# Sums of weight blocks moved from the operands' preparation into the weights' decoding, for three layers, and a later place in the queue for one token block

## The chip, the cores and the metric

The kernel runs on one core of one Trainium2 chip. The metric is device time in microseconds (us) of one execution; lower is better. Five engines work at once, each through its own instructions in a fixed order: TensorE (PE, matrix products), VectorE (DVE), ScalarE (ACT), GpSimd (POOL) and SyncE (SP), which here issues every DMA. An instruction that waits holds back all that stand behind it on its engine.

## The reference, cut to what matters

```python
x = attention(q, k, v)          # linear attention, 8 x 576 tokens, 512 wide -> x[4608, 512]
h = x @ w_in                    # 512 -> 2048
x = np.maximum(0.01 * h, h) @ w_out          # first MLP, 2048 -> 512
h = x @ w_in2                   # second MLP
out = (h * (1.0 / (1.0 + np.exp(-h)))) @ w_out2
```

The four weight matrices reach the core as 64-bit floats; the kernel turns their bits into 32-bit floats itself ("decoding"). Everything else is 32-bit.

## The kernel before, in words

**Layers and tiles.** The 4608 tokens are cut into nine token blocks `j` of 512. Layer 0 (the *plain layer*) is `x @ w_in` with 16 weight tiles `f`, run beside the attention. Layers 1, 2 and 3 are `w_out`, `w_in2` and `w_out2`. They are computed block by block with seven products in place of eight: an operand is seen as 2x2 sub-blocks, sums and differences of them are formed, and seven products `c` = 1..7 are made for each token block `j` and group `i` (four groups, `NG = 4`), always in the order `ORDER = (1, 2, 6, 7, 5, 3, 4)`. One product is 12 matmuls of 128x256, since each operand is kept as a rounded high part and a low part and three of their four combinations are summed. Below, (8,2) means token block 8, group 2.

**How an operand is made** (`operand`, `fetch`, `sums`, `split2`). Each of the seven needs a *room*, a buffer of 128x1024. Some of the seven are loaded from DRAM into their room (`fetch`, an SP DMA); the others are sums of loaded ones (`sums`, DVE, line 819, through the helper `add`). Then each is split: ACT copies it rounded into the room's first half (line 298), DVE subtracts this and writes the low part into the second half (line 294). A product can start when the DVE subtraction of both its operands is done. Weights have 28 rooms of their own (tiles `a0` to `a27`), one for each group and product; a room passes to the next layer when the last token block has used it. Token operands share 12 rooms in `r_x` (tiles `x00` to `x13`, `g`, `xs`), taken in order of need and returned after the product. Layer 1 and 3 need seven token operands for every group; layer 2 seven for a whole token block, used by all four groups.

**What comes out.** The seven products stand in PSUM banks (tiles `b`, `h`; eight in all) and are added up by `blocks`: one copy on ACT, then seven additions on DVE (line 819, `o<-o,b` and `o<-o,h`), each of which frees or helps to free a bank. In layer 1 they are written to DRAM (`x2d`) and loaded again as layer 2's token operands by `x_all`.

**Decoding the weights** (`convert`, `convert1` to `convert3`). One 128x512 tile is one 512 KB load into one of two `raw` buffers, two ACT copies (lines 331, 346) and four DVE instructions (lines 333, 337, 342, 348). Layers 1 and 2 write the decoded tile to DRAM (`w1d`, `w2d`); both buffers of `r_raw` are in use, one for the bits and one for the result. Their sums are made later, when the operand is prepared: four DVE additions of 128x512 for each group, 16 for each layer. Layer 3 (`convert3`) already makes the sums while decoding, on two tiles at a time, as four additions of 128x256 (line 410), and writes seven blocks to `w2c`, from which all seven operands are loaded. `convert2` begins when all of `convert1` is done; `convert3` when all of `convert2` is done and the last token block of layer 1 is near.

**What sets the order.** No engine chooses at run time. A planner in the kernel's code (`Queues.run`) walks through tasks, gives each operation a planned cost and picks the one that can start first; among equals the lower `rank` goes first. What it picks is written to the engines in that order. Rooms and buffers go to whoever asks first. The rank of layer `l`, block `j`, group `i` is

```python
def step2(layer, j, i):
    return NB * NF + (((layer - 1) * NB + j) * NG + i) * 2
```

so one group is two ranks. `g_all` asks for token rooms 4 ranks ahead of a group's products, `x_all` 10 ranks ahead of a token block's, the weights 8 ranks ahead.

Of the kernel before, what the change touches and what calls it, by code (L numbers as in the profile page):

```python
# [26 lines left out]
def v_tt(n):  # L27
    return 0.16 + n / 960
# [30 lines left out]
def get(ring):  # L59
    return "get", ring  # L60


class Queues:
# [26 lines left out]
    def done(self, key):  # L90
        self.events[key] = self.now
# [111 lines left out]
def linear_attention_two_mlps(  # L203
# [24 lines left out]
    nc = tc.nc  # L228
    B, H, S, D = q.shape
    NT, DM = out.shape  # L230
    DFF = w_in1.shape[1]
    P = 128
# [26 lines left out]
    w2d = tc.dram_tile([NF, P, DM], F32, name="w2d")  # L259
    w1d = tc.dram_tile([NF, P, DM], F32, name="w1d")  # L260
    w2c = tc.dram_tile([NF // 2, P, 7, DM // 2], F32, name="w2c")
# [55 lines left out]
    def load_bits(dst, l, o, f):  # L317
        yield op(("D", 1.46))
        if not o:
            dst = dst.rearrange("p (k m) -> p k m", k=KD)  # L320
        nc.sync.dma_start(out=dst, in_=w_bits(l, o, f))
# [43 lines left out]
        r_o.put(t)  # L365
        done(("w", f))

    def convert(l, o, dst, name, r):

        for f in range(NF):  # L370
            yield rank(r(f))
            raw = yield get(r_raw)
            bits = raw.bitcast(U32)
            yield from load_bits(bits, l, o, f)
            t = yield get(r_raw)
            yield from decode(bits, t[:, 0:DM], DM)
            r_raw.put(raw)
            yield op(("D", 0.73))
            nc.sync.dma_start(out=dst[f], in_=t[:, 0:DM])
            yield wait()  # L380
            r_raw.put(t)
            done((name, f))

    def convert1():
        yield wait(("l1", 1, NF - 1))
        yield from convert(0, 1, w1d, "w1", lambda f: step(3, 0) + 4 * f)

    def convert2():
        yield wait(*(("w1", f) for f in range(NF)))
        yield from convert(1, 0, w2d, "w2", lambda f: step2(1, f // 3, 0) - 4)  # L390

    def convert3():

        yield wait(*(("w2", f) for f in range(NF)), ("p", 1, NB - 2, NG - 1, 1))
        n = DM // 2
        for r in range(NF // 2):
            yield rank(step2(2, r, 0) - 4)
            t = yield get(r_raw)
# [6 lines left out]
            b = {1: t[:, 0:n], 5: t[:, n:2 * n], 2: t[:, 2 * n:3 * n], 3: t[:, 3 * n:4 * n]}  # L405
            u = yield get(r_raw)
            o = {c: u[:, i * n:(i + 1) * n] for i, c in enumerate((4, 5, 6, 7))}
            for dst, x, y in ((o[7], b[3], b[5]), (o[5], b[5], b[1]), (o[6], b[3], o[5]), (o[4], b[2], o[6])):
                yield op(("V", v_tt(n)))
                nc.vector.tensor_tensor(out=dst, in0=x, in1=y, op=ALU.subtract)  # L410
            yield op(("D", 0.73))
            nc.sync.dma_start(
                out=w2c[r, :, 0:2], in_=t.rearrange("p (c e n) -> p c e n", c=2, e=2)[:, :, 0]
            )
            yield op(("D", 0.73))
            nc.sync.dma_start(out=w2c[r, :, 2], in_=b[3])
            yield op(("D", 0.73))
            nc.sync.dma_start(out=w2c[r, :, 3:7], in_=u.rearrange("p (c n) -> p c n", c=4))
            yield wait()
            r_raw.put(t)  # L420
            r_raw.put(u)
            done(("w2c", r))

    def w_of(f):
        return wtiles[f].rearrange("p t (k m) -> p t k m", k=KD)
# [329 lines left out]
    def lend(c):  # L755
        return (yield get(r_x))

    def weights(l, i, srcs, kind, order):
# [15 lines left out]
    def weights1(i):  # L774
        w = w1d[4 * i:4 * i + 4].rearrange("(r h) p n -> h p r n", h=2)
        srcs = {
            1: w[0][:, :, 0:HB], 2: w[1][:, :, 0:HB], 5: w[0][:, :, HB:TB], 4: w[1][:, :, HB:TB]
        }
        yield from weights(1, i, srcs, "A", range(1, 8))

    def weights2(i):
        w = w2d[4 * i:4 * i + 4].rearrange("(r h) p n -> h p r n", h=2)
        srcs = {
            1: w[0][:, :, 0:HB], 2: w[0][:, :, HB:TB], 5: w[1][:, :, 0:HB], 4: w[1][:, :, HB:TB]
        }
        yield from weights(2, i, srcs, "A", range(1, 8))

    def weights3(i):
        srcs = {c: w2c[2 * i:2 * i + 2, :, c - 1].rearrange("r p n -> p r n") for c in range(1, 8)}
        yield from weights(3, i, srcs, "", ORDER)  # L790
# [187 lines left out]
    def step(j, f):  # L978
        return place[j, f]

    def step2(layer, j, i):
        return NB * NF + (((layer - 1) * NB + j) * NG + i) * 2

    with tc.manual_schedule():
# [22 lines left out]
            if f < NH:  # L1007
                spawn(f, layer0(0, f))
        spawn(0, layer0_all())
        spawn(1000, convert1())  # L1010
        spawn(1000, convert2())
        spawn(1000, convert3())
        spawn(0, later())
        for i in range(NG):
            spawn(step2(1, 0, i) - 8, weights1(i))
            spawn(step2(2, 0, i) - 8, weights2(i))
            spawn(step2(3, 0, i) - 8, weights3(i))
        spawn(step2(1, 0, 0) - 4, g_all(1))
        spawn(step2(2, 0, 0) - 10, x_all())
        spawn(step2(3, 0, 0) - 4, g_all(3))  # L1020
        spawn(step2(1, 0, 0), layers())
        qs.run()
# [30 lines left out]
```

## Time and profile before

| | |
|---|---|
| median of three runs | 1652.06 us (1650.31 to 1653.68) |
| the profiled execution | 1649.95 us |
| its span, first to last instruction | 1648.2 us |
| PE busy | 1602.6 us, 97% |
| DVE busy | 1185.9 us, 72% |
| ACT busy | 849.4 us, 52% |
| DMA queue of SP, share of 16 engines | 54.2% |

A share of the span is a mean over stages. Layer 0 ends at 528 us, layer 1 at 908, layer 2 at 1280. PE is the engine of the chain that ended last for 92% of the span; its idle time inside the layers is what can be won back, and what a change can add. A row of a timeline gives start and length; in square brackets stands how long the engine was idle before it and what released it.

### The profile page before, as it was taken

What the parts mean: (1) busy time and instruction counts of PE and PEld (TensorE: products, weight loads), DVE (VectorE), ACT (ScalarE), POOL (GpSimd) and SP (SyncE); (2) the same over time, 40 slices, a digit from 0 to 9 for tenths busy, and PEclk for the clock granted to TensorE, in tenths of its full rate; (3) what the DMA queues carried; (4) which work ended last, traced back from release to release, by engine and by line L of the source; (5) the groups of instructions that cost most, each with busy time, mean ns of one, the idle gap of its engine ahead of it and who ended that gap; (6) DMA issues with size and microseconds to landing.
All of it is one profiled execution on the core that took longest, in us unless ns stands there. A gap on an engine that the chain in (4) does not pass through costs nothing.

```text
span 1648.2 us, 30726 instructions
## 1 busy us (share of the span) xinstructions
PE 1602.6 (97%) x11456; PEld 1504.0 (91%) x11456; DVE 1185.9 (72%) x2170; ACT 849.4 (52%) x1824; POOL 41.7 (3%) x56
## 2 busy tenths in 40 slices
PE   6899999999999999999997899999999999999999
PEld 4688888888788999999996899999999999999999
DVE  8986644546335887877778888888879877777775
ACT  5768755676435444444444444444436544444442
POOL 2101000000000000000000000000000000000000
PEclk9999999999999999999997899999999999999999
DMA  8865766564556545444454455555548544444442
GB/s 225 257 187 163 209 184 187 171 206 151 173 169 212 151 152 170 153 135 129 128 168 131 147 176 189 177 179 185 184 157 273 174 132 132 132 135 136 133 137 78
DMA packets 239765, 274.66 MB, mean 167 GB/s; under 512 B 58368, under 2 KB 175104, under 8 KB 239616
## 3 DMA queue, kind: packets, MB, share of 16 engines
q1 hardware_dynamic: 239616, 272.70, 54.2%
q8 instruction: 90, 1.47, 0.4%
q14 instruction: 59, 0.48, 0.1%
HBM read 162.53 MB, written 110.10 MB: 165 GB/s over the span
## 4 chain that ended last, share of the span: by engine, by line
PE 92%; DVE 5%; DMA 1%; issue 1%; ACT 1%; SPq 0%; DVEq 0%; ACTq 0%
PE b L931 22%; PE h L931 21%; PE b L881 10%; PE h L881 10%; PE h L646 8%; PE h L648 8%; PE h L647 8%; PE a L618 2%; PE a L503 2%; DVE o L819 1%; DVE a L294 1%; PE a L603 1%; PE a L504 1%; DVE x L294 0%; DMA raw<-in_moe_w_out_dram 0%
## 5 line engine op out<-in xcount | busy, mean ns | idle before, releaser
L298 ACT ACTIVATE x<-x 128x512 fp32r<-128x512 f32 x211 | 132.9, 631 | 211.6 <-DMA x<-gd 73.1
L646 PE MATMUL h<-x,w 128*128 128x512 f32 x576 | 237.1, 412 | 3.2 <-ACT w L298 2.5
L648 PE MATMUL h<-x,w 128*128 128x512 f32 x576 | 225.5, 391 | 1.2 <-DVE w L294 1.2
L647 PE MATMUL h<-x,w 128*128 128x512 f32 x576 | 224.7, 390 | 0.7 <-DVE x L294 0.7
L819 DVE TENSOR_TENSOR o<-o,h 128x512 f32<-128x512 f32 x190 | 127.5, 686 | 50.3 <-PE h L931 20.2
L819 DVE TENSOR_TENSOR o<-o,b 128x512 f32<-128x512 f32 x188 | 126.3, 686 | 45.7 <-PE b L931 18.6
L679 ACT ACTIVATE o<-h 128x512 f32<-128x512 f32 x144 | 86.1, 598 | 139.8 <-PE h L648 135.6
L931 PE MATMUL b<-a,x 128*128 128x256 f32 x1104 | 141.6, 283 | 0.0
L893 ACT ACTIVATE o<-o 128x512 f32<-128x512 f32 x144 | 87.8, 627 | 103.8 <-DVE o L819 103.6
L294 DVE TENSOR_TENSOR x<-x 128x512 fp32r<-128x512 f32 x211 | 138.7, 685 | 2.4
L298 ACT ACTIVATE x<-o 128x512 fp32r<-128x512 f32 x166 | 103.7, 631 | 65.8 <-DVE o L819 46.3
L931 PE MATMUL b<-x,a 128*128 128x256 f32 x1008 | 129.5, 286 | 8.1 <-DVE x L294 8.1
L931 PEld LDWEIGHTS b<-a,x 128*128 128x128 f32 x1104 | 136.5, 192 | 0.3 <-DVE x L294 0.2
L646 PEld LDWEIGHTS h<-x,w 128*128 128x128 f32 x576 | 108.4, 188 | 29.7 <-ACT w L298 3.3
L881 PE MATMUL b<-x,a 128*128 128x256 f32 x1044 | 134.8, 285 | 0.0
L931 PEld LDWEIGHTS b<-x,a 128*128 128x128 f32 x1008 | 125.9, 195 | 8.3 <-DVE x L294 8.3
L648 PEld LDWEIGHTS h<-x,w 128*128 128x128 f32 x576 | 108.1, 188 | 25.7 <-DVE w L294 2.5
L881 PE MATMUL h<-x,a 128*128 128x256 f32 x1020 | 130.9, 283 | 0.0
L881 PEld LDWEIGHTS b<-x,a 128*128 128x128 f32 x1044 | 130.1, 194 | 0.0
L647 PEld LDWEIGHTS h<-x,w 128*128 128x128 f32 x576 | 108.4, 188 | 22.5 <-DVE x L294 1.4
L931 PE MATMUL h<-x,a 128*128 128x256 f32 x1008 | 126.8, 283 | 0.0
L881 PEld LDWEIGHTS h<-x,a 128*128 128x128 f32 x1020 | 126.1, 192 | 0.0
(123 smaller groups left out, 2792.0 us busy)
## 6 DMA issues: line engine op xcount, KB each, us to landing
gda<-o SPq DMA_DIRECT2D x144, 256.0 KB, 2.5
gd<-o SPq DMA_DIRECT2D x144, 256.0 KB, 2.8
x<-gd SPq DMA_DIRECT2D x102, 256.0 KB, 2.8
x<-gda SPq DMA_DIRECT2D x90, 256.0 KB, 2.9
raw<-in_moe_w_out_dram SPq DMA_DIRECT2D x32, 512.0 KB, 4.2
g<-gda SPq DMA_DIRECT2D x37, 256.0 KB, 2.7
x2d<-o SPq DMA_DIRECT2D x36, 256.0 KB, 3.2
out_dram<-o SPq DMA_DIRECT2D x36, 256.0 KB, 2.6
```

What stands on the lines that cost most here:

```text
L294: engines[e].tensor_tensor(out=out_, in0=a, in1=b.bitcast(F32), op=ALU.subtract)
L298: nc.scalar.activation(out=out_, in_=in_, func=ACTF.Copy)
L503: nc.tensor.matmul(pk[:, 0:NV], lhsT=kx[:, c * P:(c + 1) * P], rhs=vv[:, c, :], start=c == 0, stop=False)
L618: nc.tensor.matmul(po, lhsT=kv[bb, p], rhs=qT.rearrange("p (c t) -> p c t", c=4)[:, :, a:e], start=True, stop=True)
L646: nc.tensor.matmul(h, lhsT=w[:, 0, kk], rhs=x[:, 0], start=kk == 0, stop=False)
L647: nc.tensor.matmul(h, lhsT=w[:, 0, kk], rhs=x[:, 1], start=False, stop=False)
L648: nc.tensor.matmul(h, lhsT=w[:, 1, kk], rhs=x[:, 0], start=False, stop=kk == KD - 1)
L679: nc.scalar.activation(out=o, in_=h, func=ACTF.Prelu, alpha=0.01)
L819: nc.vector.tensor_tensor(out=o, in0=a, in1=b, op=alu)
L881: nc.tensor.matmul(bank[:, r * HB:(r + 1) * HB], lhsT=w4[:, a, r, k], rhs=x3[:, b, k], start=n == 0, stop=n == 5,)
L893: nc.scalar.activation(out=t, in_=t, func=ACTF.Silu)
L931: nc.tensor.matmul(bank[:, m * HB:(m + 1) * HB], lhsT=s[:, a, at:at + P], rhs=x[:, b, r * HB:(r + 1) * HB], start=i + m + n == 0, stop=i = ...
```

## The change

Three things are altered.

- **Decoding.** `convert` now decodes two tiles, makes four sums of 128x256 at once (line 396 of the changed kernel) and writes all seven blocks to DRAM, for layers 1, 2 and 3 alike (`PLANS`, `wc`). Only the bits stay in `r_raw`; the decoded tiles and the sums take four of the 16 `o` buffers, which hold activations and partial results elsewhere. The second decoder waits for three pairs of the first, the third for three pairs of the second.
- **Weights.** `weights` loads all seven operands of a group and makes no sums. Layer 2's are taken in `ORDER`, as layer 3's already were.
- **Rooms.** `x_all` asks for the rooms of layer 2's first token block 5 ranks ahead of it, not 10, and so after the last `g_all` of layer 1, which asks 6 ranks ahead by the same count.

```diff
+    PLANS = {
+        1: ({1: (0, 0), 2: (1, 0), 5: (0, 1), 4: (1, 1)}, "A", (1, 2, 4, 7, 5, 6, 3)),
+        2: ({1: (0, 0), 2: (0, 1), 5: (1, 0), 4: (1, 1)}, "A", (1, 2, 4, 7, 5, 6, 3)),
+        3: ({1: (0, 0), 5: (0, 1), 2: (1, 0), 3: (1, 1)}, "B", (1, 2, 3, 7, 5, 6, 4)),
+    }
+    def convert(l, r):
+        blocks_of, kind, order = PLANS[l]
         n = DM // 2
-        for r in range(NF // 2):
-            yield rank(step2(2, r, 0) - 4)
-            t = yield get(r_raw)
+        for pair in range(NF // 2):
+            yield rank(r(pair))
+            t = []
             for i in range(2):
                 raw = yield get(r_raw)
                 bits = raw.bitcast(U32)
-                yield from load_bits(bits, 1, 1, 2 * r + i)
-                yield from decode(bits, t[:, i * DM:(i + 1) * DM], DM)
+                yield from load_bits(bits, l // 2, l % 2, 2 * pair + i)
+                t.append((yield get(r_o)))
+                yield from decode(bits, t[i], DM)
                 r_raw.put(raw)
...
+            for i in range(2):
+                u.append((yield get(r_o)))
+                for h in range(2):
+                    dst, x, y, o = SUMS[kind][2 * i + h]
+                    to = u[i][:, h * n:(h + 1) * n]
+                    yield op(("V", v_tt(n)))
+                    nc.vector.tensor_tensor(
+                        out=to, in0=b[x], in1=b[y], op=ALU.add if o == "+" else ALU.subtract
+                    )
+                    b[dst] = to
...
+    def convert1():
+        yield wait(("l1", 1, NF - 1))
+        yield from convert(1, lambda r: step(3, 0) + 4 * r)
+    def convert2():
+        yield wait(("w", 1, 2))
+        yield from convert(2, lambda r: step2(1, r, 0) - 4)
+    def convert3():
+        yield wait(("w", 2, 2))
+        yield from convert(3, lambda r: step2(2, r, 0) - 4)
...
-        key = {1: "w1", 2: "w2", 3: "w2c"}[l]
-        yield wait(*((key, f) for f in (range(2 * i, 2 * i + 2) if l == 3 else range(4 * i, 4 * i + 4))))
-        yield from operand(("w", l, i), kind, step2(l, 0, i) - 8, order, srcs, give)
+        yield wait(("w", l, 2 * i), ("w", l, 2 * i + 1))
...
+        order = range(1, 8) if l == 1 else ORDER
+        yield from operand(("w", l, i), "", step2(l, 0, i) - 8, order, srcs, give)
     def x_all():
         for j in range(NB):
-            r = step2(2, j, 0) - 10
+            r = step2(2, j, 0) - (10 if j else 5)
```

**What the built order shows.** In the rows below a line number of the changed kernel is 9 lower for additions (810 for 819) and 2 lower for splits (292 for 294). Tiles `a` are weight rooms; `x`, `g`, `xs` token rooms; `b`, `h` banks of PSUM; `o` sums.

DVE before, layer 1's last token block: the sums and splits of layer 2's first weight group (rooms `a0` to `a6`), from the last sum to the first split of (8,2), the row of `x03`:

```order
L819 TENSOR_TENSOR o6_159<-a1_3460,o12_165 128x512
L294 TENSOR_TENSOR a0_3459<-a0_3459 128x512
L294 TENSOR_TENSOR a1_3460<-a1_3460 128x512
L819 TENSOR_TENSOR o3_156<-x02_121,x01_120 128x512
L819 TENSOR_TENSOR o9_162<-o3_156,x03_122 128x512
L819 TENSOR_TENSOR o10_163<-g_8505,o3_156 128x512
L294 TENSOR_TENSOR a2_3461<-o6_159,a2_3461 128x512
L294 TENSOR_TENSOR a3_3462<-a3_3462 128x512
L294 TENSOR_TENSOR a4_3463<-o4_157,a4_3463 128x512
L294 TENSOR_TENSOR a5_3464<-o12_165,a5_3464 128x512
L294 TENSOR_TENSOR a6_3465<-o5_158,a6_3465 128x512
L294 TENSOR_TENSOR x03_122<-x03_122 128x512
```

The first product of (8,2) waits for that last row; seven weight splits, four weight sums and three token sums stand ahead of it as one batch.

DVE in the changed kernel, the same weight group:

```order
L292 TENSOR_TENSOR a0_3546<-a0_3546 128x512
L292 TENSOR_TENSOR a1_3547<-a1_3547 128x512
L292 TENSOR_TENSOR a5_3551<-a5_3551 128x512
L810 TENSOR_TENSOR o3_156<-xs_4291,g_8662 128x512
L810 TENSOR_TENSOR o8_161<-o3_156,x10_123 128x512
L810 TENSOR_TENSOR o6_159<-x11_124,o3_156 128x512
L292 TENSOR_TENSOR x10_123<-x10_123 128x512
L292 TENSOR_TENSOR a6_3552<-a6_3552 128x512
L292 TENSOR_TENSOR x11_124<-x11_124 128x512
L292 TENSOR_TENSOR a4_3550<-a4_3550 128x512
L292 TENSOR_TENSOR g_8662<-g_8662 128x512
```

The weight sums are gone, a weight split stands beside a token split, and the first split of (8,2), `x10` on itself, is the seventh row; the splits of layer 2's first token block, which before stood ahead of all these rows, are no longer there.

DVE before, around the first addition of token block 8's outputs (`o6<-o2,b`), in (8,3); `g_8697` is the operand of the third product, `g_8729` of the fourth:

```order
L294 TENSOR_TENSOR x02_121<-x02_121 128x512
L294 TENSOR_TENSOR g_8697<-o7_160,g_8697 128x512
L342 SCALAR_TENSOR_TENSOR raw0_151<-raw1_152,raw0_151 128x512
L819 TENSOR_TENSOR o6_159<-o2_155,b_4156 128x512
L294 TENSOR_TENSOR g_8729<-o11_164,g_8729 128x512
L819 TENSOR_TENSOR o2_155<-o2_155,b_4157 128x512
L294 TENSOR_TENSOR x03_122<-o8_161,x03_122 128x512
```

DVE in the changed kernel, the same place; `g_8823` is the operand of the third product of (8,3), `x10` of the fourth:

```order
L292 TENSOR_TENSOR a10_3556<-a10_3556 128x512
L810 TENSOR_TENSOR o14_167<-o9_162,b_4293 128x512
L292 TENSOR_TENSOR g_8823<-o2_155,g_8823 128x512
L292 TENSOR_TENSOR x10_123<-o4_157,x10_123 128x512
L292 TENSOR_TENSOR x11_124<-o0_153,x11_124 128x512
```

The addition, which needs the second product of (8,3), has moved from behind the third product's split to ahead of it.

DVE before, the last addition of token block 8 (`o4<-o4,h_4750`) and what follows:

```order
L819 TENSOR_TENSOR o4_157<-o4_157,h_4750 128x512
L819 TENSOR_TENSOR o9_162<-o5_158,a14_4485 128x512
L819 TENSOR_TENSOR o14_167<-a15_4503,o9_162 128x512
L333 TENSOR_SCALAR raw0_151<-raw0_151 128x512
L337 TENSOR_SCALAR raw0_151<-raw0_151 128x512
L342 SCALAR_TENSOR_TENSOR raw0_151<-raw1_152,raw0_151 128x512
L294 TENSOR_TENSOR a14_4485<-a14_4485 128x512
L294 TENSOR_TENSOR a15_4503<-a15_4503 128x512
```

DVE in the changed kernel, the last addition (`o5<-o5,h_4958`, fed by the last product of layer 1), and behind it the seven splits of layer 2's first token block:

```order
L810 TENSOR_TENSOR o13_166<-x03_122,o1_154 128x512
L810 TENSOR_TENSOR o5_158<-o5_158,h_4958 128x512
L292 TENSOR_TENSOR x12_125<-x12_125 128x512
L292 TENSOR_TENSOR x13_126<-o15_168,x13_126 128x512
L292 TENSOR_TENSOR g_8910<-g_8910 128x512
L292 TENSOR_TENSOR xs_4291<-o7_160,xs_4291 128x512
L292 TENSOR_TENSOR x00_119<-o1_154,x00_119 128x512
L292 TENSOR_TENSOR x03_122<-x03_122 128x512
L292 TENSOR_TENSOR g_8981<-o13_166,g_8981 128x512
L292 TENSOR_TENSOR a14_4656<-a14_4656 128x512
```

These seven splits (`x12` for product 1, then 5, 3, 7, 6, `x03` for 2, `g_8981` for 4) stood in (8,1) before and now come after the last product of layer 1; the first product of layer 2 needs the first of them, its second product the sixth.

## Rows read from the trace of the kernel before

**Rows 1.** stretches, start:end and length, then busy time by engine
```profile
core 0: us, PE busy (x) PEld busy (x) DVE busy (x) ACT busy (x) POOL busy (x), PEclk, DMA share, GB/s
80.00:528.00 448.00, 448.00 (x2129) 366.93 (x2128) 238.38 (x583) 276.04 (x856) 21.80 (x20) 1.00 0.60 182
528.00:860.00 332.00, 332.00 (x2768) 331.96 (x2767) 257.94 (x418) 158.03 (x259) 0.00 (x0) 1.00 0.51 149
860.00:935.00 75.00, 56.31 (x408) 55.62 (x407) 65.58 (x109) 38.34 (x64) 0.00 (x0) 0.82 0.45 138
```
**Rows 2.** waits of PE, whole span: total us, times, longest
```profile
PE b L931 <- DVE x L294: 8.1, 1, 8.1
...
PE b L881 <- DVE o L819: 6.5, 1, 6.5
...
PE b L931 <- DVE g L294: 4.1, 1, 4.1
...
PE h L931 <- DVE xs L294: 0.5, 1, 0.5
```
**Rows 3.** timeline of PE: start, length, line, tiles, count, [idle before]
```profile
870.88 0.28 PE L931 MATMUL b<-x,a 128*128 128x256 f32 x1
...
898.15 2.76 PE L931 MATMUL b<-x,a 128*128 128x256 f32 x12
...
929.18 2.93 PE L881 MATMUL b<-xs,a 128*128 128x256 f32 x12 [6.51 <-DVE o L819]
...
934.46 1.71 PE L881 MATMUL b<-g,a 128*128 128x256 f32 x11
```
**Rows 4.** chain of waits, layer 1: start, length, engine, count
```profile
528.33 5.75 PE b L931 x48
```
**Rows 5.** timeline of DVE before the first gap
```profile
869.73 1.29 DVE L819 TENSOR_TENSOR o<-a,a 128x512 f32<-128x512 f32 x2
...
878.54 0.68 DVE L294 TENSOR_TENSOR x<-x 128x512 fp32r<-128x512 f32 x1
```
**Rows 6.** timeline of DVE in block (8,3)
```profile
901.02 0.69 DVE L819 TENSOR_TENSOR o<-o,b 128x512 f32<-128x512 f32 x1 [2.42 <-PE b L931]
901.63 0.68 DVE L294 TENSOR_TENSOR g<-o,g 128x512 fp32r<-128x512 f32 x1
```
**Rows 7.** waits of DVE, 860 to 930 us
```profile
DVE o L819 <- PE b L931: 2.4, 1, 2.4
...
DVE o L819 <- DMA x<-gda: 0.2, 1, 0.2
```
**Rows 8.** groups of DVE by form: count, busy us, mean ns
```profile
L342 DVE SCALAR_TENSOR_TENSOR raw<-raw,raw 128x512 uint32<-128x512 uint32 x48 | 33.1, 690 | 1.1
...
L333 DVE TENSOR_SCALAR raw<-raw 128x512 f32<-128x512 f32 x48 | 21.4, 445 | 33.1 <-ACT raw L331 32.4
...
L819 DVE TENSOR_TENSOR o<-a,a 128x512 f32<-128x512 f32 x16 | 10.5, 685 | 1.7 <-DMA a<-w1d 1.7
...
L410 DVE TENSOR_TENSOR raw<-raw,raw 128x256 f32<-128x256 f32 x16 | 6.7, 421 | 0.2
```
**Rows 9.** groups of ACT by form
```profile
L331 ACT ACTIVATE raw<-raw 128x512 f32<-128x512 f32 x48 | 31.9, 664 | 12.8 <-DMA raw<-in_moe_w_out_dram 6.8 <-DMA raw<-in_moe_w_in_dram 5.8
```
**Rows 10.** waits of all engines, 80 to 528 us
```profile
DVE raw L333 <- ACT raw L331: 21.7, 13, 2.8
```
**Rows 11.** DMA issues: count, KB each, median us to landing
```profile
a<-w2c SPq DMA_DIRECT2D x28, 256.0 KB, 4.6
x<-x2d SPq DMA_DIRECT2D x23, 256.0 KB, 4.0
```
**Rows 12.** waits of all engines, whole span
```profile
ACT a L298 <- DMA a<-w2c: 11.0, 8, 3.2
```
**Rows 13.** short stretches, columns as in Rows 1
```profile
50.00:60.00 10.00, 7.30 (x39) 4.75 (x39) 8.60 (x29) 9.28 (x21) 3.37 (x4) 1.00 0.99 309
...
1292.00:1293.00 1.00, 0.47 (x5) 0.27 (x3) 1.00 (x3) 0.11 (x1) 0.00 (x0) 1.00 0.75 201
```

More of the change, by code (lines that the diff above doesn't have):

```diff
@@ L258, in linear_attention_two_mlps @@
     x2d = tc.dram_tile([KD, P, NT], F32, name="x2d")
-    w2d = tc.dram_tile([NF, P, DM], F32, name="w2d")
-    w1d = tc.dram_tile([NF, P, DM], F32, name="w1d")
-    w2c = tc.dram_tile([NF // 2, P, 7, DM // 2], F32, name="w2c")
+    wc = {l: tc.dram_tile([NF // 2, P, 7, DM // 2], F32, name=f"wc{l}") for l in (1, 2, 3)}
     NG = NF // 4
@@ L366, in split1 @@
         done(("w", f))
[L368 to L374, printed above, removed]
-            t = yield get(r_raw)
[L376 to L394, printed above, removed]
+    PLANS = {
[3 rows of a table added]
+    }
+    def convert(l, r):
+        blocks_of, kind, order = PLANS[l]
         n = DM // 2
-        for r in range(NF // 2):
-            yield rank(step2(2, r, 0) - 4)
-            t = yield get(r_raw)
+        for pair in range(NF // 2):
+            yield rank(r(pair))
+            t = []
             for i in range(2):
@@ L401, in convert3 @@
                 bits = raw.bitcast(U32)
-                yield from load_bits(bits, 1, 1, 2 * r + i)
-                yield from decode(bits, t[:, i * DM:(i + 1) * DM], DM)
+                yield from load_bits(bits, l // 2, l % 2, 2 * pair + i)
+                t.append((yield get(r_o)))
+                yield from decode(bits, t[i], DM)
                 r_raw.put(raw)
-            b = {1: t[:, 0:n], 5: t[:, n:2 * n], 2: t[:, 2 * n:3 * n], 3: t[:, 3 * n:4 * n]}
-            u = yield get(r_raw)
@@ L407, in convert3 @@
[L407 to L415, printed above, removed]
@@ L416, in convert3 @@
-            nc.sync.dma_start(out=w2c[r, :, 2], in_=b[3])
-            yield op(("D", 0.73))
-            nc.sync.dma_start(out=w2c[r, :, 3:7], in_=u.rearrange("p (c n) -> p c n", c=4))
-            yield wait()
-            r_raw.put(t)
-            r_raw.put(u)
-            done(("w2c", r))
+            b = {c: t[i][:, h * n:(h + 1) * n] for c, (i, h) in blocks_of.items()}
+            u = []
+            for i in range(2):
[8 more added lines that the diff above has]
+                    b[dst] = to
@@ new lines, in convert @@
+            for i in range(2):
+                kept = [c for c in order[:3] if blocks_of[c][0] == i]
+                at, h = order.index(kept[0]), blocks_of[kept[0]][1]
+                yield op(("D", 0.73))
+                nc.sync.dma_start(
+                    out=wc[l][pair, :, at:at + len(kept)],
+                    in_=t[i][:, h * n:(h + len(kept)) * n].rearrange("p (c n) -> p c n", n=n),
+                )
+                yield op(("D", 0.73))
+                nc.sync.dma_start(
+                    out=wc[l][pair, :, 3 + 2 * i:5 + 2 * i], in_=u[i].rearrange("p (c n) -> p c n", c=2)
+                )
@@ L424, in w_of @@
+            yield wait()
+            for x in t + u:
+                r_o.put(x)
+            done(("w", l, pair))
+    def convert1():
[7 more added lines that the diff above has]
+        yield from convert(3, lambda r: step2(2, r, 0) - 4)
     def w_of(f):
@@ L756, in lend, with weights @@
         return (yield get(r_x))
-    def weights(l, i, srcs, kind, order):
+    def weights(l, i):
         def give(c):
@@ L768, in give @@
             return slot[("w", l - 1, i), c]
-        key = {1: "w1", 2: "w2", 3: "w2c"}[l]
-        yield wait(*((key, f) for f in (range(2 * i, 2 * i + 2) if l == 3 else range(4 * i, 4 * i + 4))))
-        yield from operand(("w", l, i), kind, step2(l, 0, i) - 8, order, srcs, give)
-    def weights1(i):
-        w = w1d[4 * i:4 * i + 4].rearrange("(r h) p n -> h p r n", h=2)
+        yield wait(("w", l, 2 * i), ("w", l, 2 * i + 1))
         srcs = {
-            1: w[0][:, :, 0:HB], 2: w[1][:, :, 0:HB], 5: w[0][:, :, HB:TB], 4: w[1][:, :, HB:TB]
+            c: wc[l][2 * i:2 * i + 2, :, at].rearrange("r p n -> p r n") for at, c in enumerate(PLANS[l][2])
         }
[L779 to L790, printed above, removed]
+        order = range(1, 8) if l == 1 else ORDER
+        yield from operand(("w", l, i), "", step2(l, 0, i) - 8, order, srcs, give)
     def x_all():
         for j in range(NB):
-            r = step2(2, j, 0) - 10
+            r = step2(2, j, 0) - (10 if j else 5)
             yield rank(r)
@@ L1009, in linear_attention_two_mlps @@
         spawn(0, layer0_all())
-        spawn(1000, convert1())
-        spawn(1000, convert2())
-        spawn(1000, convert3())
+        for t in (convert1, convert2, convert3):
+            spawn(1000, t())
         spawn(0, later())
         for i in range(NG):
-            spawn(step2(1, 0, i) - 8, weights1(i))
-            spawn(step2(2, 0, i) - 8, weights2(i))
-            spawn(step2(3, 0, i) - 8, weights3(i))
+            for l in (1, 2, 3):
+                spawn(step2(l, 0, i) - 8, weights(l, i))
         spawn(step2(1, 0, 0) - 4, g_all(1))
-        spawn(step2(2, 0, 0) - 10, x_all())
+        spawn(step2(2, 0, 0) - 5, x_all())
         spawn(step2(3, 0, 0) - 4, g_all(3))
```

## The prediction

> **What bounds the kernel now.** I read the busy time by stage first, then PE's waits, then PE and DVE in order of time around the waits. In layer 0 after its first 80 us (80 to 528) and in most of layer 1 (528 to 860) PE is busy for 448.00 of 448 us and 332.00 of 332 us; the reader is to see that nothing there can be won. In 860:935, where layer 1 hands over to layer 2, it is busy for 56.31 of 75 us, at a mean granted clock of 0.82, while DVE is busy for 65.58 [rows 1]. PE's waits of the whole span say the same: after the start-up there are three that count, 8.1, 6.5 and 4.1 us, all on DVE, and one of 0.5 us at the next hand-over [rows 2].
>
> What they cost with all that follows: the first product of (8,2) starts at 870.88, the sixth of layer 2's group (0,1) at 934.46 [rows 3]. Between the two starts lie 7 + 7 + 7 + 5 = 26 products. At full rate 48 matmuls, which are four products, take 5.75 us [rows 4], so one takes 1.44 and 26 take 37.4. The 63.6 us that passed are **26.1 us too many**: 18.7 in the three waits, most of the rest in products that ran at half rate behind them, as the one at 929.18 with 2.93 us for its 12 matmuls [rows 3].
>
> Why DVE: ahead of the first wait it works through the batch of weight sums, weight splits and token sums without a pause, from 869.73 to the split at 878.54, with which PE goes on [rows 5]. I take a longer stretch to see if this is load or order. From the first product of (8,1), which is 7 x 1.44 us before 870.88, so at 860.8, to the product at 929.18 there are 31 products, 44.6 us of PE at full rate. In the built order DVE has 100 instructions there: 16 weight sums, 24 weight splits, 26 token splits, 13 token sums, 9 additions of outputs, and 12 of the third decoding. Back to back, a 128x512 one follows another after 0.61 us (901.02 to 901.63) [rows 6]; with the decoding's shorter ones the hundred need about 59.5. DVE's own waits add 8.3, eight rows from 2.4 down to 0.2 [rows 7]. That makes 67.8, and 68.4 passed. So DVE is the bound of this stretch and of no other.
>
> **The change part by part.**
>
> *Load at the hand-over.* The 16 weight sums and the 12 decoding instructions go, three weight splits come in: 75 instructions, all of 128x512, at 0.61 us [rows 6] 45.7 us against 44.6 of PE. DVE no longer needs more than PE; what is left is set by the order, and I walk through the three places in it.
>
> (a) The first addition of block 8's outputs waits for the second product of (8,3), and the split for the third product now stands behind it. Before, that addition began at 901.02, 0.11 us after the product's end (898.15 + 2.76), and the next instruction 0.61 later [rows 3, 6]; a split takes 0.68 and PE goes on 0.05 later [rows 2, 5]. PE waits 0.11 + 0.61 + 0.69 + 0.05 = 1.5 us.
>
> (b) The last addition waits for layer 1's last product, and the seven splits of layer 2's first token block stand behind it. Its first product waits 1.5 in the same way. Its second needs the sixth split: 0.11 + 6 x 0.61 + 0.69 + 0.05 = 4.5 after layer 1's end, where PE would be there after 1.5 + 1.44 = 2.9: 1.6 more.
>
> (c) From there to the addition that frees the bank for the fourth product of (0,1) the order has 30 DVE instructions: the end comes 0.11 + 29 x 0.61 + 0.69 + 0.05 = 18.5 us after layer 1's end; PE would be there after 4.5 + 9 x 1.44 = 17.5: 1.0 more.
>
> Together **5.6 us** in place of 26.1. From below: the counts alone leave 45.7 - 44.6 = 1.1, and nothing excludes that DVE runs ahead by that much, so 0. From above: DVE's 8.3 us of waits [rows 7] come back on top of the load, 9.4, with one more loss of half-rate products, 2.5 as behind the wait at 929.18: 12. I take the walk, since it uses the new order.
>
> *Where the work goes.* Up to the end of layer 0 the built order has 51 more decoding instructions (12.75 tiles), 72 sums of 128x256 and 15 fewer weight sums. A tile costs two instructions of 0.69 and two of 0.44; a 256-wide sum 0.42; a weight sum 0.685 [rows 8]: 28.9 + 30.3 - 10.3 = 49 us of DVE. It has 448 - 238 = 210 us free there [rows 1]. ACT gets 26 copies of 0.664 [rows 9], 17 us, of 172 free. SP gets 46 stores, 12 loads of bits and 11 of operands more, 19 MB: 42 GB/s on the 182 of this stretch, a DMA share of 0.74 in place of 0.60 [rows 1]. The cover for all this is that PE waited for nobody in this stretch although DVE waited 21.7 us for 13 of its decodings [rows 10]; and the attention's outputs stand, in both orders, 47 or more steps of PE (most of them three matmuls of layer 0) ahead of their use from the third token block on. If that cover failed: 12 more loads, each with 21.7 / 26 = 0.83 us of wait on PE, 10 us. A gain is excluded, PE being full. I take 0.5, near the row's zero.
>
> *The first hand-over.* In layer 1's last weight group the seventh operand is now loaded instead of summed, into a room that comes free only with layer 0's last product, at 528.3 [rows 4]. With a landing of 4.6 us [rows 11], ACT's copy of 0.66 and five DVE instructions (the weight split, three token sums and the first token split of (0,1), 3.1 us) that token operand is ready near 536.7; its product is due seven products after 528.3, at 538.4. Cost 0; if the load lands 2 us later, 1. I take 0.5.
>
> *Layer 2 and the second hand-over.* 84 instructions of the third decoding leave layer 2. PE did not wait for them, so nothing comes back. The hand-over from layer 2 to layer 3 keeps its order and its 0.5 us [rows 2].
>
> *Sum.* 1649.95 - 26.1 + 5.6 + 0.5 + 0.5 = 1630.4 for a run like the profiled one, which lay 2.1 below the median of the three; against the median **1632.5**.
>
> **The rivals.**
>
> *The decoding is paid in layer 0 (slower).* The second and third decoder now run beside the first; attention's small products stand in PE's own order, and one that waits for a held-up DVE holds layer 0. At 2.8 us, the longest of these waits [rows 10], for each of 12 more loads, PE loses 34 us: 1632.5 + 33 = 1665. It turns to slower once 55 decodings cost PE more than 24 us, 0.44 each; 43 cost it nothing before. 0.05.
>
> *Last to take rooms, last to be ready.* The loads of layer 2's first token block wait for rooms of (8,2). If they come late, load 4.0 [rows 11], ACT 0.6 and eleven DVE instructions, 6.7, all stand behind layer 1's end: 11.3 in place of the 3.1 of (b), with a half-rate restart of 2.4: 10.6 more, 1643. For it: the load of weights is now 22 in this stretch, not 14. Against: three of the four loads stand 9 to 11 products, over 13 us, ahead of their use. 0.12.
>
> *The change does not shorten the hand-over as it says, because loads set it.* ACT waited 11.0 us for 28 weight loads of layer 3 [rows 12], and PE lost 0.5 at that place. If here 22 loads cost 22/28 of it and all reaches DVE, which has no slack: 8.6 more, 1641. 0.08.
>
> *Short gaps hold the clock down.* Four gaps of 1.0 to 1.6 us lie within 15 products. If PE ran them at half rate, that is 15 x 1.44 = 21.6 more, 1654, no gain. Against: the 0.5 us gap at 1292 has a granted clock of 1.00 around it, and so has 50:60, where PE was busy for 7.30 of 10 us [rows 13]. 0.04. The Trainium skill, page "TensorE: Matmul & The Clock Gate", section "A second HAM failure mode: psum-queue depth-cycling", tells of a kernel in which short idle times between groups of matmuls made the clock swing between its levels; by that rule this case is the one to come, and the two stretches just named do not show it.
>
> **How the numbers follow.** The forecast, 1632.5, has 0.71 and by its own bounds reaches from 1626 (all of 26.1 won) to 1640. With the two cases at 1641 and 1643 taken in, 1626 to 1643 leaves out about 0.1, and some tail. A difference under 0.2%, 3.3 us, is about what a measurement of this kernel can't tell from none. Faster: the forecast and the two cases above, 0.91, of which I take off 0.03 for what I did not see; slower 0.06; the same 0.06.
>
> **What would show it.** Right: in the 75 us around the hand-over PE's waits are three or four, none over 2 us, and the clock stays at 1.00; DVE's lines there have no sums of `a`; layer 0 ends within 2 us of 528; line 396 appears 96 times at 0.42. Wrong: a wait of PE over 4 us on a token split of layer 2's first block, waits of PE on attention tiles between 80 and 528, or a clock under 1.00 at the hand-over.

## The result, and the profile after

The changed kernel takes **1632.88 us** (median of four, 1630.06 to 1636.52) against 1651.18 for the kernel before, run beside it on the same chip: a ratio of 0.989, 95% interval 0.986 to 0.992. The forecast was 1632.5, in a range of 1626 to 1643. Time and most places came out as forecast; one step of the reasoning did not, and the experiments show which.

The profiled execution is one of 1635.08 us, its span 1633.1. The same stretches as in [rows 1], of the changed kernel: start:end and length, then busy time of PE, PEld, DVE, ACT and POOL, the granted clock, DMA share, GB/s.

```profile
80.00:528.00 448.00, 448.00 (x2127) 366.83 (x2127) 287.91 (x698) 290.96 (x880) 19.31 (x17) 1.00 0.72 223
528.00:860.00 332.00, 331.15 (x2734) 329.52 (x2734) 266.16 (x443) 160.59 (x263) 0.00 (x0) 1.00 0.55 165
860.00:935.00 75.00, 70.80 (x584) 69.99 (x583) 68.56 (x113) 44.61 (x75) 0.00 (x0) 1.00 0.62 198
```

In layer 0 DVE has 49.5 us more than before, ACT 15 more, the DMA share is 0.72, and PE is still full. At the hand-over PE is busy for 70.80 of 75 us in place of 56.31, at a clock of 1.00 in place of 0.82. PE's waits in 860 to 935 us (total, times, longest), which answer to [rows 2]:

```profile
PE b L922 <- DVE g L292: 1.3, 1, 1.3
PE b L872 <- DVE x L292: 1.3, 1, 1.3
PE h L872 <- DVE x L292: 1.3, 1, 1.3
PE b L872 <- DVE o L810: 0.3, 1, 0.3
```

Four waits of 4.2 us in all stand where three of 18.7 stood. Their places, in PE's timeline (start, length, line, tiles, count, [idle before]):

```profile
891.50 1.58 PE L922 MATMUL b<-g,a 128*128 128x256 f32 x11 [1.33 <-DVE g L292]
...
900.23 1.57 PE L872 MATMUL h<-x,a 128*128 128x256 f32 x11 [1.27 <-DVE x L292]
...
903.24 3.01 PE L872 MATMUL b<-x,a 128*128 128x256 f32 x23 [1.32 <-DVE x L292]
...
916.60 1.69 PE L872 MATMUL b<-xs,a 128*128 128x256 f32 x12 [0.27 <-DVE o L810]
```

These are the third product of (8,3), the first and second of layer 2, and the fourth of (0,1). None is followed by a slow product: the eleven matmuls that are left of a product take 1.57 us. A product's first matmul runs ahead of the wait (the row of 0.28 at 898.68 below), since it needs only the high parts; the wait is for the low part.

**A measure for all that follows.** I take the start of the first product of each layer from PE's timeline; for the changed kernel:

```profile
532.12 3.04 PE L922 MATMUL b<-g,a 128*128 128x256 f32 x24
...
898.68 0.28 PE L872 MATMUL h<-x,a 128*128 128x256 f32 x1
...
1265.17 3.04 PE L922 MATMUL b<-a,x 128*128 128x256 f32 x24
```

A layer has 252 products, 362.9 us at 1.44 each. What layers 1 and 2 take beyond that is their loss, waits and slow products together. All values in us, from the profiled execution of each kernel but for the last column:

| kernel | layer 0 ends | loss, layer 1 | loss, layer 2 | both | median time |
|---|---|---|---|---|---|
| before | 528.2 | 17.1 | 9.3 | 26.4 | 1651.18 |
| changed | 532.1 | 3.7 | 3.6 | 7.3 | 1632.88 |
| changed, again | 530.1 | 3.1 | 3.6 | 6.7 | 1633.68 |
| rooms only | 529.8 | 6.3 | 14.3 | 20.5 | 1644.14 |
| sums only | 532.3 | 17.5 | 0.0 | 17.5 | 1644.95 |
| third decoder late | 531.8 | 1.6 | 11.9 | 13.5 | 1639.88 |
| sums made four times | 532.5 | 3.8 | 6.9 | 10.7 | 1639.09 |
| sums only, later weights | 530.0 | 17.4 | 0.0 | 17.4 | 1643.74 |
| later weights | 527.9 | 1.5 | 1.9 | 3.4 | 1631.18 |
| later weights, second operand early | 527.8 | 2.0 | 1.5 | 3.5 | 1628.26 |

The medians were taken on several chips, on which the kernel before took 1648.3 to 1651.5, so rows of different experiments are compared by their losses, and the ratios below are each to the kernel before on the same chip. The end of layer 0 moves by almost 5 us between these executions, by 2 between the two of the changed kernel; the last section shows where.

### The profile page after: what moved, and what is told of

It is laid out like the page before. It is cut to its first block, busy times and chain, and to the rows that moved or that the text cites. A ratio compares the mean times of both kernels' runs of the same rounds, so it can differ in the third digit from the quotient of the medians.

```text
span 1633.1 us, 30896 instructions
## 1 busy us (share of the span) xinstructions
PE 1603.1 (98%) x11456; PEld 1501.8 (92%) x11456; DVE 1194.2 (73%) x2205; ACT 851.3 (52%) x1824; POOL 39.1 (2%) x53
## 4 chain that ended last, share of the span: by engine, by line
PE 93%; DVE 5%; DMA 1%; issue 0%; ACT 0%; SPq 0%; DVEq 0%; ACTq 0%
PE b L922 22%; PE h L922 21%; PE b L872 11%; PE h L872 11%; PE h L651 8%; PE h L653 8%; PE h L652 8%; PE a L623 2%; PE a L508 2%; PE a L608 1%; DVE o L810 1%; PE a L509 1%; DVE a L292 1%; DVE x L292 1%; DVE g L292 0%
## 5 line engine op out<-in xcount | busy, mean ns | idle before, releaser
L922 PE MATMUL b<-x,a 128*128 128x256 f32 x1044 | 132.0, 284 | 0.6 <-DVE x L292 0.5
L922 PEld LDWEIGHTS b<-x,a 128*128 128x128 f32 x1044 | 128.1, 192 | 1.1 <-DVE x L292 1.0
L872 PEld LDWEIGHTS h<-x,a 128*128 128x128 f32 x1008 | 124.9, 192 | 1.5 <-DVE x L292 1.5
L872 PE MATMUL b<-x,a 128*128 128x256 f32 x960 | 123.8, 283 | 1.3 <-DVE x L292 1.3
L922 PEld LDWEIGHTS h<-x,a 128*128 128x128 f32 x996 | 122.3, 192 | 0.7 <-DVE x L292 0.6
```

The costliest lines, as they stand in the source:

```text
L872: nc.tensor.matmul(bank[:, r * HB:(r + 1) * HB], lhsT=w4[:, a, r, k], rhs=x3[:, b, k], start=n == 0, stop=n == 5,)
L922: nc.tensor.matmul(bank[:, m * HB:(m + 1) * HB], lhsT=s[:, a, at:at + P], rhs=x[:, b, r * HB:(r + 1) * HB], start=i + m + n == 0, stop=i = ...
```

## Experiments

**1. The rooms alone.** The kernel before, with the later place alone (the task that asks starts 5 ranks ahead, too).

```diff
-            r = step2(2, j, 0) - 10
+            r = step2(2, j, 0) - (10 if j else 5)
```

> The kernel before, with only the rooms changed: the first token block of layer 2 asks for its rooms 5 ranks ahead, not 10. Theory (load): in the 31 products around the hand-over VectorE keeps its 100 instructions, 59.5 us against 44.6 us of products, so the waits only move, from the first products of (8,2) and (8,3) to later places, the largest of 7 to 9 us at the bank of the fourth product of (0,1); they add up to 15 to 20 us as before, and the time stays between 1641 and 1653. Rival (order): the batch of splits ahead of (8,2) was the cause, and putting the seven splits of the token block behind it brings most of the gain: waits under 8 us together, time under 1638.

Measured: ratio to before 0.9967 (0.9951 to 0.9984), a third of the gain. PE's waits (whole span):

```profile
PE b L881 <- DVE o L819: 8.2, 1, 8.2
...
PE b L931 <- DVE g L294: 3.1, 1, 3.1
...
PE b L881 <- DVE x L294: 1.3, 1, 1.3
PE h L881 <- DVE x L294: 1.3, 1, 1.3
PE b L931 <- DVE x L294: 1.2, 2, 0.9
```

15.1 us of waits, and the largest moved to the bank of the fourth product of (0,1), as the load theory said. But the waits of 8.1 and 4.1 at the first products of (8,2) and (8,3) are gone, and layer 1 lost 6.3 in place of 17.1: here the rival had a point, though its limits (under 8 us of waits, under 1638) were missed by far.

**2. The sums alone.** The changed kernel, with the rooms as before (the start of the task, too).

```diff
-            r = step2(2, j, 0) - (10 if j else 5)
+            r = step2(2, j, 0) - 10
```

> The changed kernel with the rooms as before: layer 2's first token block asks 10 ranks ahead again. Theory (load): the sums and the decoding are gone from the hand-over, and that is nearly all of the gain; VectorE has 5 additions of outputs more there than in the changed kernel, because nothing stands behind them, and the waits of TensorE are two, at the first products of (8,2) and (8,3), about 4 and 3 us, 7 to 8 together against 4.2 in the changed kernel: 1632 to 1638. Rival (order): the rooms carry half of the gain or more, waits over 12 us, time 1642 or more.

Measured: ratio 0.9961 (0.9947 to 0.9976). The load theory fell. VectorE has no weight sums and no decoding left in the stretch, and still:

```profile
PE b L922 <- DVE x L292: 6.3, 1, 6.3
PE b L922 <- DVE g L292: 5.4, 1, 5.4
```

Layer 1 loses 17.5 us, as before the change; layer 2 loses nothing. The cause stands in the timelines of DVE and of SP, here of this kernel:

```profile
875.03 3.69 DVE L292 TENSOR_TENSOR a<-a 128x512 fp32r<-128x512 f32 x6
879.70 0.69 DVE L810 TENSOR_TENSOR o<-x,x 128x512 f32<-128x512 f32 x1 [0.98 <-DMA x<-gda]
```
```profile
870.71 0.33 SPq L718 DMA_DIRECT2D x<-gda  x1
...
875.03 0.33 SPq L718 DMA_DIRECT2D x<-gda  x1
```

and of the changed kernel:

```profile
861.74 0.42 SPq L718 DMA_DIRECT2D x<-gda  x1
...
866.20 0.46 SPq L718 DMA_DIRECT2D xs<-gda  x1
```

These are the first and the last of the four token loads of (8,2). With the rooms as before, layer 2's first token block takes seven of the twelve rooms early, and (8,2) gets rooms only as the products of (8,1) give them back: each of the four loads is issued within 0.2 us of the end of one of them. The last is issued at 875.03, and the first product of (8,2) is due at 876.4. That product's own operand is loaded first, but its split overwrites it in place and so waits for the sum that reads it; that sum builds on another, which needs the last load. VectorE finishes six weight splits and then waits for that load. (8,3) repeats it: its last load is issued at 893.72 for a product due at 895.09, VectorE waits 0.66 for it, and TensorE 5.4. In the changed kernel the loads of (8,2) are issued 9 us earlier. The kernel before had the same lateness, which shows in SP's timeline:

```profile
868.08 1.76 SPq L713 DMA_DIRECT2D x<-gda  x2
```

These are its last two loads of (8,2), for a product due at 870.88 [rows 3]. There VectorE had the batch of weight sums and splits to do while they came [rows 5]. Batch and late loads stood side by side; with the batch gone the loads alone make a wait of 6.3 in place of 8.1.

**3. Are the weight splits ahead of (8,2) to blame?** Experiment 2, with layer 2's weights asking later as well.

```diff
-        yield from operand(("w", l, i), "", step2(l, 0, i) - 8, order, srcs, give)
+        yield from operand(("w", l, i), "", step2(l, 0, i) - (4 if l == 2 else 8), order, srcs, give)
```

> The changed kernel with two edits: the rooms as before (10 ranks ahead), and the weights of layer 2 asking 4 ranks ahead in place of 8, which moves their splits behind the token splits that are due sooner. With the rooms as before alone, TensorE waited 6.3 and 5.4 us at the first products of (8,2) and (8,3) and layers 1 and 2 took 17.5 us over full rate. Theory (rooms): the token loads of (8,2) are issued only as the products of (8,1) give rooms back, from 870.7 us on there, so that the splits of the weights ahead of them are not the cause; both waits stay at 5 us or more, 14 to 18 us over full rate, 1640 to 1646. Rival (the weight splits ahead are the cause): with them moved back both waits fall under 3 us and the time under 1636.

Measured: waits of 5.6 and 5.3 us, layer 1 loses 17.4, ratio 0.9951 (0.9931 to 0.9972). As a test of the rival the edit is weak: six weight splits still ran ahead of (8,2), from 872.51 on. What answers the rival is the row behind them, where VectorE again waited for a load, so that without the splits this sum could not have begun sooner:

```profile
877.23 0.69 DVE L810 TENSOR_TENSOR o<-x,x 128x512 f32<-128x512 f32 x1 [1.02 <-DMA x<-gda]
```

**4. The third decoder late again.**

```diff
-        yield wait(("w", 2, 2))
+        yield wait(("w", 2, 2), ("p", 1, NB - 2, NG - 1, 1))
```

> The changed kernel, in which the third decoder waits for the end of the products of (7,3) in layer 1 again, as before the change; sums and rooms stay changed. 12 instructions of decoding, about 6.7 us of VectorE, return to the 31 products around the hand-over, and 84 to layer 2. Theory (load): waits there go from 4.2 to 9 to 13 us, most of it at the bank of the fourth product of (0,1); 1637 to 1643. Rival (the decoding of layer 3 fits into pauses of VectorE, and only the weight sums counted): waits stay under 6 us, 1631 to 1635. Layer 0, with 43 instructions of decoding and sums less than the changed kernel, should not become shorter under either; if it does by over 2 us, the decoding there was not hidden.

Measured: ratio 0.9939 (0.9917 to 0.9960). The three waits of 1.3 us stay, and the bank wait of 0.3 becomes

```profile
PE b L872 <- DVE o L810: 6.8, 1, 6.8
```

6.5 us more for twelve instructions worth 6.7: at this place VectorE's work counts in full, as the theory said. Without 43 instructions of decoding and sums layer 0 ended at 531.8, not 532.1, after a start-up with the same clock to within 0.02, and PE was busy for 448.00 of 448 us with them and without; so there they had cost nothing.

**5. Layer 0's cover.** Each decoding sum is made four times over.

```diff
-                    yield op(("V", v_tt(n)))
-                    nc.vector.tensor_tensor(
-                        out=to, in0=b[x], in1=b[y], op=ALU.add if o == "+" else ALU.subtract
-                    )
+                    for _ in range(4):
+                        yield op(("V", v_tt(n)))
+                        nc.vector.tensor_tensor(
+                            out=to, in0=b[x], in1=b[y], op=ALU.add if o == "+" else ALU.subtract
+                        )
```

> The changed kernel, with each of the 96 sums of 128x256 in the decoding made four times over, into the same place. Up to the end of layer 0 VectorE has 152 such sums more and 39 instructions of decoding less, about 43 us more work; in layers 1 and 2 it has 60 and 76 sums more. Theory (layer 0 hides VectorE's work until it is full): busy VectorE in 80 to 528 us goes from 288 to about 330 of 448, TensorE keeps 448 of 448, layer 0 ends where it did, and the time stays within 4 us of the changed kernel's. Rival (layer 0 pays once VectorE's share passes some point): waits of TensorE on attention tiles appear in 80 to 528 and layer 0 ends over 5 us later; by 0.44 us for each extra decoding-sized piece of work 1645 or more.

Measured, for 80 to 528 and for layer 2:

```profile
80.00:528.00 448.00, 448.00 (x2128) 366.70 (x2127) 327.94 (x809) 281.58 (x865) 26.12 (x24) 1.00 0.66 204
935.00:1264.00 329.00, 326.24 (x2717) 325.84 (x2716) 279.75 (x479) 152.72 (x260) 0.00 (x0) 1.00 0.52 177
```

Layer 0 hid another 40 us of VectorE: 328 busy of 448, PE full, its end at 532.5. The median rose by 6 us, 2 more than the theory allowed; of the 3.4 us that the trace shows, 3.3 are in layer 2, in two waits of 0.9 and 1.8 on additions of outputs. (The changed kernel's profiled execution lies 2.2 above its median, so less shows here than between the medians.) Layer 0 did not pay; layer 2 did, where this kernel has 76 more sums.

**6. Which waits cost more than themselves?** The changed kernel, with one wait of a chosen length in each of seven undisturbed token blocks of layer 1.

```diff
+    HOLD = {1: 9, 2: 2, 3: 7, 4: 3, 5: 5, 6: 4, 7: 1}
+    def hold(j):
+        key = ("x", 1, j, NG - 1)
+        yield wait(("op", key, 6))
+        for _ in range(HOLD[j]):
+            yield op(("V", v_tt(TB)))
+            sub("V", slot[key, 6][:, 1], made[key, 6], slot[key, 6][:, 0])
...
+        done(("hold", j))
...
         yield from add(t, s, p)
         end(2)
+        if key[0] == 1 and key[1] in HOLD:
+            yield from hold(key[1])
...
+                    if l == 1 and j in HOLD and i == NG - 1 and c == 6:
+                        yield wait(("hold", j))
```

The last two lines let the third product of the block's last group wait for the repeated splits.

> The changed kernel, in which seven of layer 1's undisturbed token blocks get a wait of a chosen length: behind the first addition of the block's outputs, which itself waits for the second product of the last group, the split of that group's third operand is made n times again. n is 9, 2, 7, 3, 5, 4, 1 in blocks 1 to 7; by step (a) of the prediction TensorE then waits 0.85 + 0.61 n there: 6.3, 2.1, 5.1, 2.7, 3.9, 3.3, 1.5 us. Theory (the length of one wait decides): the waits up to about 3 us cost only themselves, with the granted clock at 1.00 behind them and 1.44 us for a product; from 3 to 4 us on the products behind run at half rate for a while, 1 to 3 us more for each. Rival 1 (time lost is time waited): every product behind a wait takes 1.44 us, so that 25 us of waits cost 25. Rival 2 (the short gaps too hold the clock down): products behind the waits of 1.5 and 2.1 us take over 2 us.

Measured (PE's timeline; the rows behind a wait follow it where they are needed):

```profile
614.07 6.50 PE L940 MATMUL b<-x,a 128*128 128x256 f32 x35 [7.15 <-DVE x L292]
620.40 3.04 PE L940 MATMUL h<-x,a 128*128 128x256 f32 x24
...
658.74 1.95 PE L940 MATMUL b<-g,a 128*128 128x256 f32 x11 [2.06 <-DVE g L292]
...
665.96 5.92 PE L940 MATMUL h<-x,a 128*128 128x256 f32 x48
...
887.61 1.57 PE L940 MATMUL b<-x,a 128*128 128x256 f32 x11 [1.34 <-DVE x L292]
889.02 5.92 PE L940 MATMUL h<-x,a 128*128 128x256 f32 x48
```

The granted clock behind three of the waits:

```profile
614.00:616.00 2.00, 1.93 (x9) 1.93 (x10) 1.82 (x4) 1.25 (x2) 0.00 (x0) 0.50 0.00 0
660.00:662.00 2.00, 2.00 (x12) 2.00 (x11) 1.76 (x3) 0.64 (x2) 0.00 (x0) 0.50 0.10 36
887.00:889.00 2.00, 1.39 (x11) 1.39 (x12) 2.00 (x4) 0.75 (x2) 0.00 (x0) 1.00 0.41 135
```

A clock of 0.50 is the lower of the two levels, 1.2 GHz. I compare the distance between two row starts with 0.12 us for each matmul in between. Behind 7.15 us: 6.33 for 35 matmuls, 2.1 lost. Behind 2.06: 7.22 for 47, 1.6 lost. Behind 1.34: 1.41 for 11, 0.1 lost. In the same way the waits of 5.69, 4.24, 3.51 and 2.79 lost 2.0, 2.3, 1.4 and 1.6. In sum 26.8 us of waits and 11 us behind them, 38; the one time measured, 1671.69, lies 38 above the changed kernel's. Rival 1 fell. Rival 2 held for the wait of 2.06 and not for that of 1.34. The theory had the right kind and the wrong point: it put the turn at 3 to 4 us. A wait of 1.85 in experiment 5 left the clock at 1.00, one of 2.06 here did not. The turn is not a length alone: in the start-up one and the same wait of 2.08 us was followed by the low clock in some executions and not in others (last section). In these seven blocks the cost behind a wait hardly grows with its length: 1.4 to 2.3 us from 2.06 to 7.15.

**7. The order that is left.** The changed kernel with layer 2's weights later (the edit of experiment 3), then with the second operand of layer 2's first token block second in line as well:

```diff
-            yield from operand(("x", 2, j), "B", r, (1, 5, 3, 7, 6, 2, 4), srcs, lend)
+            yield from operand(("x", 2, j), "B", r, (1, 5, 3, 7, 6, 2, 4) if j else (1, 2, 5, 3, 6, 7, 4), srcs, lend)
```

> The changed kernel as it is, as the measure for the two that follow: 1630 to 1636, by whether the start-up loses clock between 50 and 80 us.

> The changed kernel, with the weights of layer 2 asking 4 ranks ahead in place of 8, so that VectorE makes their splits behind the token splits that are due sooner; each weight room has 28 products, 40 us, between its last use and its next. Same instructions, another order. Theory (at 45.7 us of work for 44.6 of products the order decides): the waits at the third product of (8,3), at layer 2's first product and at the bank of the fourth product of (0,1) go, one of 1.85 us at layer 2's second product is left (sixth split, as in (b)): 4.2 us of waits become about 1.9, time 2 us below the changed kernel's, 0.1%. Rival (the later weights come too late): a wait on a weight split appears in token block 0 of layer 2, and the time is the same or 1 to 3 us longer.

> As the kernel with the later weights, and the second operand of layer 2's first token block is made second, not sixth. Theory: one wait of 1.5 us is left, at layer 2's first product; 2.7 us below the changed kernel. Rival (later weights come too late): as for the kernel with the later weights alone.

Measured: the loss of both layers falls from 6.7 to 3.4 and 3.5 us. With later weights one wait of 1.6 is left at the hand-over, at layer 2's second product; with both edits one of 1.3, at its first. The second version runs in 1626.11 to 1630.98 (five runs, median 1628.26) against 1632.12 to 1635.33 (six runs, median 1633.68) for the changed kernel on the same chip; ratio to before 0.9875 (0.9855 to 0.9896). It beats both kernels. 3.2 us of the 5.4 between the medians are the loss in layers 1 and 2; most of the rest lies in where layer 0 ended, 2.3 earlier in the profiled execution, which no edit here touches.

## Why the prediction was right, and where not

**What bounds the kernel now.** 26.1 us too many at the hand-over; the measure above gives 26.4 for both layers. Right. The reading of why was half right: VectorE's load set the wait of 6.5 at the bank (experiments 1 and 4), but the waits of 8.1 and 4.1 stay nearly as long without it, because the rooms hold them too. The prediction took one sum over the whole stretch, 67.8 us of work and waits for 68.4 passed, as proof that DVE was the bound. It counted DVE's own waits, 8.3 [rows 7], as its load; one of the rows left out of that group is

```profile
DVE o L819 <- DMA x<-x2d: 1.7, 1, 1.7
```

a load of layer 2's first token block, the one that took the rooms.

**The step that failed** is *Load at the hand-over*: "what is left is set by the order" was true of the new rooms alone. Experiment 2 has the forecast's reduced work, plus a few additions, and loses 17.5 us. By the prediction's argument that version would have come out near the changed kernel; it came out 12 us above. The total was right because the walk of the three places used the order with both edits in it. That the median lies within 0.4 us of 1632.5 is luck in part: the four runs spread over 6.5 us, and the profiled one lies 4.7 above the 1630.4 that the prediction gives for a run like the profiled one before, 3.9 of it in where layer 0 ended.

**The two edits need each other.** Rooms alone win 6 us, sums alone 6, both 18. Rooms alone take 10.8 off layer 1 and add 5.0 to layer 2, where the load now shows. Sums alone take 9.3 off layer 2 and leave layer 1 as it was. Only together are the waits short, and then the products behind them cost nothing: before, about 7 of the 26.4 us were products at the lower clock.

**The walk.** (a) 1.5, measured 1.33. (b) 1.5 and 1.6, measured 1.27 and 1.32. (c) 1.0, measured 0.27. In (a) and (b) the excess is mostly the 0.12 us of the first matmul, which doesn't wait. The rows of DVE for (a), answering to [rows 6]:

```profile
890.16 0.69 DVE L810 TENSOR_TENSOR o<-o,b 128x512 f32<-128x512 f32 x1 [1.03 <-PE b L922]
890.77 0.68 DVE L292 TENSOR_TENSOR g<-o,g 128x512 fp32r<-128x512 f32 x1
```

The addition, the split 0.61 later, PE 0.05 after it: as walked. A wait of DVE itself, 1.03, stands ahead of it, so it was ahead of PE there, and the wait is the order's.

**Layer 0.** +49 us of DVE forecast, +49.5 measured; line 396 has 72 + 24 instructions of 423 and 418 ns. Hidden, as forecast; experiment 5 shows 40 us more of room. That layer 0 ends within 2 us of 528 was wrong in this execution, 532.1, for a reason outside the change (below).

**The first hand-over.** 0.5 forecast, and PE did wait 0.52 us at 543.00, but not for the seventh weight. DVE had split that at 536.65 and then stood idle for token loads:

```profile
536.65 0.68 DVE L292 TENSOR_TENSOR a<-a 128x512 fp32r<-128x512 f32 x1
540.32 0.69 DVE L810 TENSOR_TENSOR o<-x,x 128x512 f32<-128x512 f32 x1 [2.99 <-DMA x<-gda]
```

Right size, wrong cause.

**Not foreseen:** three gaps of 0.35 to 0.45 us in layer 1, for instance

```profile
652.40 6.37 PE L922 MATMUL h<-x,a 128*128 128x256 f32 x48
658.61 1.60 PE L922 MATMUL b<-x,a 128*128 128x256 f32 x12
```

where 48 matmuls should take 5.76 and 6.21 passed. They stand near 658, 740 and 820 us in the changed kernel and in the sums-only version, and not in the kernel before, with the rooms alone or with the third decoder late. So they go with that decoder's place in layer 1. The list of waits does not have them; the chain of the work that ended last shows what PE waits for:

```profile
656.46 0.69 DVE x L292
657.15 0.04 issue
657.20 1.58 PE h L922 x11
```

PE goes on when a token split of the next block is done. That split stands on VectorE behind the block's last addition and three other splits, and the addition waits for PE itself: the same pattern as in (a). The other two gaps show it as well.

**The rivals.** *Layer 0 pays* fell with experiments 4 and 5. *Last to be ready*: the first product of layer 2 waited 1.27, no more than in (b). *Loads set the hand-over* fell for the weights' loads; with the rooms as before, token loads do set it (experiment 2). *Short gaps hold the clock down* fell for the hand-over: four gaps of 0.3 to 1.3 us within 25 us, clock 1.00. It was nearer than its chance of 0.04 said: 2.06 us was enough in experiment 6, and in the start-up of the changed kernel the clock fell with no wait over 1.1 us just before (last section). The prediction took 50 to 60 us in one profile, at 1.00, as a sign against it; in other executions that stretch had 0.66. The Trainium skill, page "TensorE: Matmul & The Clock Gate", section "A second HAM failure mode: psum-queue depth-cycling", tells of a kernel in which frequent short idle times made the clock swing; the start-up agrees in some executions, the hand-over of the changed kernel does not.

## What to carry to other kernels

Where two engines are almost equally loaded, the sum of work over a stretch doesn't tell which wait has which cause: follow each wait back to the issue of the load behind it, and ask who held its buffer. Judge an edit by the longest wait that it leaves: in layers 1 and 2 every wait of 2.06 us or more also slowed the products behind it, while several of 1.3 us didn't. Work with a late deadline, here weight splits that had 40 us, can go behind work that is due now; that gave another 3 us, and no wait on a weight split appeared.

## What the hardware showed

**The clock's drop can come after work has begun again.** Behind the wait of 2.06 us, at 658.74, the clock was 0.89 in the first 1.3 us and 0.50 in the two after it; a look at the first product alone misses most of the cost. Behind the wait of 7.15 us, which ended at 614.07, it was low before work began:

```profile
658.70:660.00 1.30, 1.26 (x9) 1.26 (x10) 1.30 (x3) 0.61 (x1) 0.00 (x0) 0.89 0.32 109
612.00:614.00 2.00, 0.00 (x0) 0.00 (x0) 1.93 (x4) 0.00 (x0) 0.00 (x0) 0.50 0.00 0
```

**The length of a wait does not decide alone.** About 65 us into the kernel one matmul waits 2.08 us. In the kernel before:

```profile
65.75 0.50 PE L646 MATMUL h<-x,w 128*128 128x512 f32 x1 [2.08 <-ACT w L298]
60.00:70.00 10.00, 7.64 (x36) 5.62 (x37) 9.61 (x22) 9.05 (x21) 1.14 (x1) 1.00 1.11 346
```

and with the rooms alone, which change nothing there:

```profile
65.72 0.50 PE L646 MATMUL h<-x,w 128*128 128x512 f32 x1 [2.08 <-ACT w L298]
67.00:70.00 3.00, 3.00 (x10) 2.44 (x9) 2.64 (x6) 2.03 (x5) 0.00 (x0) 0.56 1.16 288
```

What decides between the two, no run here shows.

**The start-up can lose the clock, in some executions and not in others.** From 50 to 70 us the granted clock was 1.00 in the profile before ([rows 13] and the row above), and in the changed kernel's:

```profile
50.00:60.00 10.00, 8.71 (x34) 6.37 (x35) 6.47 (x22) 6.84 (x16) 3.19 (x3) 0.66 0.85 270
60.00:70.00 10.00, 7.79 (x30) 4.76 (x30) 9.50 (x23) 9.12 (x21) 1.31 (x1) 0.75 1.04 333
```

PE's instructions are the same in both kernels there. The changed kernel waits 1.03 us at 50.34 and 0.94 at 51.61, and from 52 us on the clock is 0.50; before, waits of 1.07 and 0.95 at the same two places left it at 1.00. The two later-weights versions had 1.00 and ended layer 0 at 527.8 and 527.9; kernels with the drop ended it at 529.8 to 532.8. That is up to 5 us, as much as the whole difference that experiment 7 looks for, so small changes are better compared by the lengths of layers than by one time.
